# Turning V by 32x32 block transposes and a trip through DRAM instead of by TensorE transposes

## The chip, the cores and the metric

The kernel runs on one core of a Trainium2 chip. A core has a matrix engine (TensorE, called PE in the profile, with its weight loads as PEld), a vector engine (VectorE, DVE), a scalar engine (ScalarE, ACT), GpSimd (POOL) and SyncE (SP), which here only issues DMA transfers. Each engine works through its own instructions in their order and waits for others by semaphores. Work is in SBUF (128 partitions), matmul results land in PSUM banks, weights and inputs lie in DRAM. The metric is the time of one execution on the device, in microseconds (us); lower is better.

## The reference

Four layers in a row, A, B, A, B, each as x + layer(layernorm(x)), on x of 2048 tokens by 640.

Layer A is an attention with a recurrent memory. The tokens are cut into 64 segments of 32. For each segment the 8 memory rows and the 32 tokens make a sequence of 40:

```python
for s in range(n_seg):
    h = concatenate([mem, x[segment s]])            # 40 x 640
    q, k, v = h @ Wq, h @ Wk, h @ Wv                # 32 heads of 192
    p = softmax(mask(q @ k.T / sqrt(192)))
    o = (p @ v) @ Wo                                # 40 x 640
    mem = o[:8]; out[segment s] = o[8:]
```

The memory of a segment is the output of the segment before, so the 64 segments of one A layer follow each other. Layer B is a dilated sliding-window attention (window 8, dilation 2, 32 heads of 20). Weights and activations are bf16.

## The kernel before, in words

The two A layers use the same weights, and the two passes through A and B run side by side, two segments apart (LAG = 2): a step t handles segment t of the first A layer in lane 0 and segment t - 2 of the second in lane 1, 40 columns each, so NT = 80 columns. There are 64 segments and so 66 steps, and one more for the end of layer B. In steps 2 to 63, 62 in all, both lanes are at work; steps 0, 1, 64 and 65 have one lane.

A step goes through the 32 heads in 8 quads of 4 heads (768 columns of each of Wq, Wk, Wv). For quad i, `step` emits: K (`a_k`: `proj`, 30 matmuls of 128x128 weights by 80 columns, L297, then ScalarE copies into KF and Kz), Q (`a_q`, VectorE copy into QT, L316), P.V of the quad before (`a_pv`), V (`a_v`: 30 matmuls, VectorE copy into vT, L342), the output projection of the quad five back (`a_o`, L415), the normalisation of the quad before (`a_norm`, VectorE, L398 to L400), the scores S (`a_s`, L363, L364, then the exponential on ScalarE, L366) and the mask (`a_mask`, VectorE, L372). Pieces of layer B for the segment before stand between them. Quad 7 has a tail of its own: the last P.V, and the output projections of quads 3 to 7, whose result gives the memory rows of the next step.

All projections leave their result transposed: head columns on partitions, tokens along the free axis. P.V needs V with tokens on partitions. `a_vt` turns it: six PE transposes of 128 columns (L351) into one PSUM bank and one VectorE copy to Vt (L353), emitted after K of the next quad, for each of the 8 quads of a two-lane step. In one-lane steps most quads compute V with tokens on partitions at once (`a_v_rows`, L331).

P.V (L384) takes Vt as weights, with columns of ones for the sums of the softmax. ScalarE forms logarithm and exponential of these sums (R, L388, L390) and VectorE multiplies (`a_norm`).

The order on every engine, SP included, is the order of emission (a manual schedule). An instruction waits for all that it needs, and those behind it on its engine wait too.

The weights of layer A are 64 halves of 128x1920 (two for each quad and each of K, Q, V, O). 41 of them stay in SBUF; `resident_halves` picks the other 23, evenly over the step by PE work, and these are loaded again in every step into a ring of 4 buffers. `used` frees a buffer when its half has been used last, and `prefetch` then emits the next load on SP, in two pieces of 240 KB (L249), each of which waits for PE to be done with the buffer. The DMAs of SP take eight completion semaphores in turn. The loads of x (L652) and the stores of the result (L655) go through the ACT queue.

Of the kernel before, what the change touches and what calls it, by code (L numbers as in the profile page):

```python
# [28 lines left out]
LAG = 2  # L29
OLAG = 5  # L30
EPS = 1e-5

# [10 lines left out]
N_HALVES = 64  # L43
N_RES = 41
RING = 4
# [3 lines left out]

def half_order():  # L50

    quad = 15 * (NT + MM)
    other = [2 * NX * NC, 2 * NC * NC * NX, NC * NC * NX + 18 * NX, NC * P + 18 * NX, 8 * NX, 8 * NX,
             3 * P + NC * NC * NX, 2 * NX * NC]
    order = []
    for i in range(NQUAD):
        for kind in "kqv":
            order += [((kind, i, h), quad) for h in range(2)]
        last = order.pop()
        order.append((last[0], last[1] + 16 * (NT + MM) + 6 * (P + MM) + other[i]))  # L60
        for j in ([i - OLAG] if i < NQUAD - 1 else range(i - OLAG, NQUAD)):
            if j >= 0:
                order += [(("o", j, h), quad) for h in range(2)]
    return order
# [14 lines left out]
class Kernel:  # L79
    def __init__(self, ctx, tc, A_x, A_mem0, A_Wq, A_Wk, A_Wv, A_Wo, B_wqkv, B_wo, out):  # L80
        self.tc = tc
        self.nc = tc.nc
        self.x = A_x
        self.mem0 = A_mem0
        self.out = out
        self.n_seg = A_x.shape[0]
        self.wsrc = {"k": A_Wk, "q": A_Wq, "v": A_Wv, "o": A_Wo}
        pool = lambda name, bufs, **kw: ctx.enter_context(tc.tile_pool(name=name, bufs=bufs, **kw))
        self.cp = pool("consts", 1)
        self.wres = pool("wres", 1)  # L90
        self.wring = pool("wring", RING)
        self.ap1 = pool("act1", 1)
        self.ap2 = pool("act2", 2)
        self.bp = pool("bact", 1)
        self.ebp = pool("ebp", 4)
        self.otp = pool("otp", OLAG)
        self.xp = pool("xio", 1)
        self.ps_big = pool("ps_big", 1, space=PSUM)
        self.ps_one = pool("ps_one", 1, space=PSUM)
        self.ps_two = pool("ps_two", 1, space=PSUM)  # L100
        self.units = {}
        order = half_order()
        self.resident = resident_halves(order)
        streamed = [u for u, _ in order if u not in self.resident]
        self.kept = streamed[:4]
        self.kept_uses = {u: 0 for u in self.kept}
        second = streamed[4:7] + [("b", part, 0) for part in range(3)] + streamed[7:8] + [("b", 3, 0)] + streamed[8:]
        self.loads = [u for u, _ in order] + second + streamed * (self.n_seg + LAG - 2)
        self.ring_free = RING
        self.n_loaded = 0  # L110
        self.B_wqkv, self.B_wo = B_wqkv, B_wo
        self.build_consts()

    def build_consts(self):
# [23 lines left out]

        self.hT = pers("hT", [P, NC * NT + 88], 1)[0]
        self.KF = pers("KF", [P, 4 * NT + 48], 1)[0]  # L140
        self.Kz = pers("Kz", [P, 4 * NT + 48], 1)[0]
        self.Vt = pers("Vt", [P, 2 * VH], 1, zero=False)[0]
        nc.vector.memset(self.Vt[:], 1.0)
        self.vT = pers("vT", [P, 6 * NT + 48], 1)[0]
        nc.vector.memset(self.xin[0][:, 1], 0.0)
        nc.vector.memset(self.xin[1][:], 0.0)
# [139 lines left out]
    def proj(self, kind, i, t):  # L286
# [4 lines left out]
        w = [self.units[kind, i, h] for h in range(2)]  # L291
        mem_last = kind == "k" and i == 0
        order = [(n, c) for c in range(NC) for n in range(6)] if mem_last else [(n, c) for n in range(6) for c in range(NC)]
# [29 lines left out]
    def a_v_rows(self, i, t):  # L323

        nc = self.nc
        w = [self.units["v", i, h] for h in range(2)]
        vt = self.Vt[0:NT, :].rearrange("p (a b c) -> p a b c", a=2, b=2)
        for h in (1, 0):
            ps = self.big("ps_vr", ((2, 3) if i == 1 else (0, 2))[1 - h])
            for c in range(NC):  # L330
                nc.tensor.matmul(ps[:, 0:2 * DH], lhsT=self.hT[:, NT * c:NT * c + P], rhs=w[h][:, c, :], start=(c == 0), stop=(c == NC - 1))  # L331
            (nc.scalar.copy if i == 0 and h else nc.vector.tensor_copy)(out=vt[:, h, :, 0:DH], in_=ps[0:NT, 0:2 * DH].rearrange("p (b c) -> p b c", b=2))
        self.used("v", i)

    def a_v(self, i, t):
# [4 lines left out]
        nc = self.nc  # L340
        ps = self.proj("v", i, t)
        nc.vector.tensor_copy(out=self.cols(self.vT[:, 0:6 * NT].rearrange("p (a n) -> p a n", a=6)), in_=self.cols(ps[:, 0:6 * NT].rearrange("p (a n) -> p a n", a=6)))  # L342

    def a_vt(self):

        if self.v_rows:
            return
        nc = self.nc
        ps = self.ps_big.tile([P, 6, P], BF16, name="ps_vt", tag="bank2")
        for n in range(6):  # L350
            nc.tensor.transpose(out=ps[:, n, :], in_=self.vT[:, NT * n:NT * n + P], identity=self.ident[:])  # L351
        vt = self.Vt
        nc.vector.tensor_copy(out=vt[0:NT, :].rearrange("p (a b c) -> p a b c", a=2, b=2)[:, :, :, 0:DH],  # L353
                              in_=ps[0:NT].rearrange("p (a b) c -> p a (b c)", a=2).rearrange("p a (b c) -> p a b c", b=2))

# [18 lines left out]

    def a_pv(self):


        nc = self.nc
        em, vt = self.em, self.Vt
        ops = self.ps_two.tile([P, 2, 512], F32, name="ps_o", tag="o")  # L380
# [441 lines left out]
    def step(self, t):  # L822
# [4 lines left out]
        if t == T:  # L827
            return self.b_alone(b)
        for i in range(NQUAD - 1):
            self.a_k(i, t)  # L830
            if b is not None and i == 6:
                self.b_norm(1)
            if i >= 1:
                self.a_vt()
            if b is not None and i == 1:
# [6 lines left out]
            if b is not None:  # L842
                self.b_first(b, i)
            if i >= 1:
                self.a_pv()
            if b is not None and i == 6 and self.one_lane():
                self.b_ot()
            self.a_v(i, t)
            if b is not None:
                self.b_second(b, i)  # L850
            if i >= OLAG:
                self.a_o(i - OLAG)
# [5 lines left out]
            if b is not None and i == 0:  # L858
                self.b_ln(b)
            self.a_mask()  # L860
            if b is not None and i == 0:
                self.b_ln_rstd()
# [10 lines left out]
        self.a_k(7, t)  # L873
        self.a_vt()
        self.a_q(7, t)
        if nt < T:
            self.ln1_sums(nt)
        self.a_pv()
        self.a_v(7, t)
        self.a_o(7 - OLAG)  # L880
        self.a_norm(6)
        self.a_s()
        self.a_vt()
        self.a_mask()
        self.a_o(8 - OLAG)
        self.a_o(9 - OLAG, slice(0, NC), False)
        if nt < T:
            self.ln1(nt)
        self.a_pv()
        if nt < T:  # L890
# [53 lines left out]
def _lay_out(name, a):  # L944
# [3 lines left out]
    if name == "A_mem0":  # L948
        return a.reshape(NM, NC, P).transpose(2, 1, 0)
    if name in ("A_Wq", "A_Wk", "A_Wv"):  # L950
        return a.reshape(NC, P, NQUAD, 2, QE // 2).transpose(2, 1, 3, 0, 4).reshape(NQUAD, P, 2 * HALF)
# [37 lines left out]
```

## Time and profile before

| | |
|---|---|
| median of the runs (3) | 3126.81 us, 3123.92 to 3128.7 |
| profiled execution: span | 3128.7 us; no other time of it is listed |
| PE busy, PEld busy | 98%, 97% |
| DVE, ACT, POOL busy | 76%, 59%, 18% |
| mean share of the 16 DMA engines between 1000 and 2000 us | 0.76 to 0.78 |
| PE transposes of V (ps_vt, L351) | 5% of the chain, 504 groups of six |
| VectorE copies vT (L342), Vt (L353) | 653 ns and 554 ns, 504 times each |
| weight pieces on SP (240 KB) | 3.7 to 4.0 us to landing, median by tensor |
| granted clock | 0.993 |

The times of the runs are device times. The profile is one execution; its span is from its first to its last instruction. "Busy" is the time in which an engine has an instruction at work. In lines of groups and of the timeline, a name such as `vT<-ps_v` is the tile written and the tile read, an L number is the line of the kernel, and "x6" merges six instructions; the start of the next line on an engine, not the end of one, tells its rate, since instructions overlap. A name such as w_ring<-in_A_Wv_dram is a DMA. The chain is followed back from the last instruction to what each one waited for.

### The profile page before, as it was taken

How to read it: one execution, taken by the hardware profiler on the slowest of the kernel's cores; microseconds unless marked ns; L12 is line 12 of the kernel's file. 1: busy time of each engine (PE TensorE's matmuls, PEld its weight loads, DVE VectorE, ACT ScalarE, POOL GpSimd, SP SyncE). 2: the span in 40 equal slices, each digit the busy share in tenths (PEclk: the TensorE clock that was granted, in tenths of full speed). 3: DMA queues.
4: the chain of work that ended last, by engine and by line, in shares of the span. 5: the costliest groups of instructions: out<-in, count | busy, mean ns of one | idle time of the engine just before them, and what ended most of it. 6: DMA issues, size and time to landing. Idle time of an engine off the chain costs nothing.

```text
span 3128.7 us, 187179 instructions
## 1 busy us (share of the span) xinstructions
PE 3079.1 (98%) x83454; PEld 3030.8 (97%) x83454; DVE 2369.5 (76%) x6009; ACT 1845.1 (59%) x5612; POOL 553.2 (18%) x1028
## 2 busy tenths in 40 slices
PE   6999999999999999999999999999999999999998
PEld 4899999999999999999999999999999999999997
DVE  3677777777777777777777777777777777877776
ACT  2556656656656656656656656656656656655654
POOL 2111111111111111111111111111111111111121
PEclk7999999999999999999999999999999999999999
DMA  9877777777777777777777777777777777777776
GB/s 392 287 246 248 246 246 239 250 243 246 249 244 249 246 246 250 247 247 247 247 246 248 248 245 249 250 246 245 250 246 248 249 244 249 250 243 250 248 251 219
DMA packets 452970, 785.02 MB, mean 251 GB/s; under 512 B 58560, under 2 KB 444352, under 8 KB 452160
## 3 DMA queue, kind: packets, MB, share of 16 engines
q1 hardware_dynamic: 438480, 767.84, 76.4%
q8 instruction: 652, 10.68, 1.4%
q10 hardware_dynamic: 13680, 5.21, 0.7%
q14 instruction: 158, 1.29, 0.1%
HBM read 770.22 MB, written 2.62 MB: 247 GB/s over the span
## 4 chain that ended last, share of the span: by engine, by line
PE 96%; DMA 3%; issue 1%; ACT 0%; DVE 0%; SPq 0%; ACTq 0%
PE ps_k L297 18%; PE ps_acc L415 18%; PE ps_q L297 17%; PE ps_v L297 17%; PE ps_vt L351 5%; PE ps_o L384 5%; PE ps_s L363 2%; PE ps_s L364 2%; PE ps_bs L581 2%; PE ps_bk L529 2%; PE ps_by L640 2%; PE ps_bq L529 1%; PE ps_bv L529 1%; PE ps_vr L331 1%; PE ps_bo L607 1%
## 5 line engine op out<-in xcount | busy, mean ns | idle before, releaser
L388 ACT ACTIVATE R<-ps_o 64x160 f32<-64x160 f32 (+1 forms) x2112 | 620.1, 294 | 338.4 <-PE ps_o L384 122.8
L297 PEld LDWEIGHTS <-w_ring 128*128 128x128 bf16 x16470 | 676.6, 100 | 18.7 <-issue 5.3
L297 PE MATMUL ps_q<-hT,w_q 128*128 128x80 bf16 (+1 forms) x12870 | 541.1, 201 | 4.8 <-DMA w_q<-in_A_Wq_dram 4.2
L566 POOL TENSOR_TENSOR QX<-QB,hmask 128x448 bf16<-128x448 bf16 (+2 forms) x325 | 304.5, 945 | 1338.2 <-ACT QB L544 1025.1
L297 PEld LDWEIGHTS <-w_q 128*128 128x128 bf16 x12870 | 493.8, 100 | 6.0 <-DMA w_q<-in_A_Wq_dram 5.3
L309 ACT CAST KF<-ps_k 128x320 bf16<-128x320 f32 (+1 forms) x528 | 218.5, 414 | 414.7 <-PE ps_k L297 399.1
L415 PE MATMUL ps_acc<-OT,w_o 128*128 128x80 bf16 (+1 forms) x9900 | 458.9, 201 | 3.7 <-DMA w_o<-in_A_Wo_dram 2.3
L342 DVE CAST vT<-ps_v 128x480 bf16<-128x480 f32 (+1 forms) x504 | 329.3, 653 | 166.2 <-PE ps_v L297 148.1
L316 DVE CAST QT<-ps_q 128x480 bf16<-128x480 f32 (+1 forms) x528 | 337.5, 639 | 119.7 <-PE ps_q L297 116.5
L297 PE MATMUL ps_v<-hT,w_v 128*128 128x80 bf16 (+1 forms) x9480 | 423.7, 201 | 4.1 <-issue 2.4
L415 PEld LDWEIGHTS <-w_o 128*128 128x128 bf16 x9900 | 393.2, 100 | 5.4 <-DMA w_o<-in_A_Wo_dram 2.9
L297 PE MATMUL ps_k<-hT,w_k 128*128 128x80 bf16 (+1 forms) x7920 | 373.5, 201 | 2.9 <-DMA w_k<-in_A_Wk_dram 2.7
L297 PEld LDWEIGHTS <-w_v 128*128 128x128 bf16 x9480 | 371.6, 100 | 4.9 <-issue 2.9
L297 PE MATMUL ps_k<-hT,w_ring 128*128 128x80 bf16 (+1 forms) x7860 | 370.5, 201 | 5.4 <-issue 3.4
L366 ACT ACTIVATE E<-ps_s 80x320 bf16<-80x320 f32 (+1 forms) x528 | 220.7, 418 | 241.4 <-PE ps_s L364 240.1
L398 DVE TENSOR_TENSOR OT<-ps_o,R 128x320 bf16<-128x320 f32 (+1 forms) x528 | 254.1, 481 | 135.4 <-ACT R L390 115.7
L297 PEld LDWEIGHTS <-w_k 128*128 128x128 bf16 x7920 | 321.5, 100 | 3.7 <-DMA w_k<-in_A_Wk_dram 3.1
L353 DVE COPY Vt<-ps_vt 80x768 bf16<-80x768 bf16 x504 | 279.0, 554 | 56.4 <-PE ps_vt L351 44.5
L415 PE MATMUL ps_acc<-OT,w_ring 128*128 128x80 bf16 (+1 forms) x5940 | 307.9, 201 | 1.5 <-issue 1.1
L297 PE MATMUL ps_v<-hT,w_ring 128*128 128x80 bf16 (+1 forms) x5640 | 264.8, 202 | 0.8 <-DMA w_ring<-in_A_Wv_dram 0.7
L372 DVE TENSOR_TENSOR E<-E,maskA 80x320 bf16<-80x320 bf16 (+1 forms) x528 | 207.0, 392 | 64.7 <-ACT E L366 54.0
L390 ACT ACTIVATE R<-R 128x320 f32<-128x320 f32 (+1 forms) x528 | 244.1, 462 | 16.7
(159 smaller groups left out, 4932.2 us busy)
## 6 DMA issues: line engine op xcount, KB each, us to landing
w_ring<-in_A_Wk_dram SPq DMA_DIRECT2D x1036, 240.0 KB, 3.7
w_ring<-in_A_Wo_dram SPq DMA_DIRECT2D x780, 240.0 KB, 3.8
w_ring<-in_A_Wv_dram SPq DMA_DIRECT2D x776, 240.0 KB, 4.0
w_ring<-in_A_Wq_dram SPq DMA_DIRECT2D x390, 240.0 KB, 4.0
w_q<-in_A_Wq_dram SPq DMA_DIRECT2D x5, 960.0 KB, 11.0
w_v<-in_A_Wv_dram SPq DMA_DIRECT2D x6, 480.0 KB, 11.3
w_ring<-in_A_Wk_dram SPq DMA_DIRECT2D x6, 480.0 KB, 10.2
w_ring<-in_A_Wo_dram SPq DMA_DIRECT2D x6, 480.0 KB, 11.3
```

Of the source, the lines that this page charges most:

```text
L297: nc.tensor.matmul(ps[:, NT * n + self.c0:NT * n + self.c1], lhsT=w[n // 3][:, c, P * (n % 3):P * (n % 3 + 1)], rhs=hT[:, NT * c + self.c0 ...
L309: nc.scalar.copy(out=kf, in_=pv[:, :, 0:3:2, :])
L316: self.nc.vector.tensor_copy(out=self.cols(qt[:]), in_=self.cols(ps[:, 0:6 * NT].rearrange("p (a n) -> p a n", a=6)))
L342: nc.vector.tensor_copy(out=self.cols(self.vT[:, 0:6 * NT].rearrange("p (a n) -> p a n", a=6)), in_=self.cols(ps[:, 0:6 * NT].rearrange("p ...
L353: nc.vector.tensor_copy(out=vt[0:NT, :].rearrange("p (a b c) -> p a b c", a=2, b=2)[:, :, :, 0:DH], in_=ps[0:NT].rearrange("p (a b) c -> p ...
L366: nc.scalar.activation(out=self.cols(e[0:NT]), in_=self.cols(sv[0:NT]), func=ACT.Exp, scale=float(DH) ** -0.5)
L372: nc.vector.tensor_tensor(out=self.cols(e[0:NT]), in0=self.cols(e[0:NT]), in1=self.cols(self.maskA[0:NT, :]).unsqueeze(1).to_broadcast([NT ...
L388: nc.scalar.activation(out=self.cols(r[r0:r0 + 64, :, j]), in_=self.cols(src), func=ACT.Ln)
L390: nc.scalar.activation(out=rf, in_=rf, func=ACT.Exp, scale=-1.0)
L398: nc.vector.tensor_tensor(out=oc[:, :, 0:3:2], in0=ov[:, :, 0:4:3], in1=r, op=ALU.mult)
L415: nc.tensor.matmul(self.cols(acc[:, k]), lhsT=w[m // 3][:, m % 3, P * c:P * (c + 1)], rhs=self.cols(ot[:, m]), start=(i == 0 and m == 0 an ...
L566: self.nc.gpsimd.tensor_tensor(out=qx[:, 0:nh, self.on], in0=self.qb[:, c, self.on].unsqueeze(1).to_broadcast([P, nh, n]), in1=self.hmask[ ...
```

## The change

In two-lane steps, V of quads 2 to 7 is turned in another way. The V projection runs two quads ahead: V of quad 2 at the start of the step, V of quad i + 2 in quad i. Its PSUM result is copied to vS (one buffer). `v_blocks` turns 32x32 blocks on VectorE, 128 partitions by 576 elements, from vS into vB (one buffer). `v_send` stores vB to a DRAM buffer (two buffers), and `v_fetch` brings it back in three loads, of token rows 0 to 31, 32 to 63 and 64 to 79, in runs of 192 elements, straight into Vt, of which there are now two buffers. The store and the three loads are issued on SP. Quads 0 and 1 keep the PE transposes. So that the loads have long runs, the columns of Wv of quads 2 to 7 are reordered on the host, and one-lane steps write their V in the same order.

One resident half less fits, 40 instead of 41, so that 24 halves are streamed per step; two-lane steps stream them in the order of the new use.

```diff
-N_RES = 41
+N_RES = 40
...
+        if two_lanes:
+            units = [("v", VLAG)] * (i == 0) + [("k", i), ("q", i)]
+            units += [("v", VLAG + i)] * (1 <= i < NQUAD - VLAG) + [("v", i)] * (i < VLAG)
...
+        self.v_by_dma = not self.one_lane() and i >= VLAG
+        if self.v_by_dma:
+            nc.vector.tensor_copy(out=self.vS[:, 0:6 * NT], in_=ps[:, 0:6 * NT])
+            return
...
+    def v_blocks(self, i):
+        src = self.vS[:]
+        src = bass.AP(src.tensor, src.offset, [list(src.ap[0]), [VB, 3], [NT, 6], [1, VB]])
+        self.nc.vector.transpose(out=self.vB[:].rearrange("p (b n c) -> p b n c", b=3, n=6), in_=src)
+
+    def v_send(self, i):
+        self.v_sent[i] = self.vdp.tile([P, 3 * DH], BF16, name="v_rows")
+        self.nc.sync.dma_start(out=self.v_sent[i][:], in_=self.vB[:])
+
+    def v_fetch(self, i):
+        rows = self.v_sent.pop(i)[:].rearrange("(h i) c -> i h c", h=4)
+        for b in range(3):
+            n = min(VB, NT - VB * b)
+            vt = self.Vts[i % 2][VB * b:VB * b + n, :].rearrange("p (h c) -> p h c", h=4)
+            self.nc.sync.dma_start(out=vt[:, :, 0:DH], in_=rows[0:n, :, DH * b:DH * (b + 1)])
...
+        ahead = not self.one_lane()
+        if ahead:
+            self.a_v(VLAG, t)
         for i in range(NQUAD - 1):
             self.a_k(i, t)
+            if ahead and i == 0:
+                self.v_blocks(VLAG)
...
             self.a_q(i, t)
...
+            if ahead and i >= 1:
+                self.v_send(i + 1)
             if i >= 1:
-                self.a_pv()
+                self.a_pv(i - 1)
...
-            self.a_v(i, t)
+            if not ahead or i == 0:
+                self.a_v(i, t)
+            elif i < NQUAD - VLAG:
+                self.a_v(i + VLAG, t)
             if b is not None:
                 self.b_second(b, i)
+            if ahead and i == 1:
+                self.a_v(i, t)
...
             self.a_mask()
+            if ahead and 1 <= i < NQUAD - VLAG:
+                self.v_blocks(i + VLAG)
+            if ahead and i >= 1:
+                self.v_fetch(i + 1)
...
-        self.a_v(7, t)
+        if not ahead:
+            self.a_v(7, t)
```

## The prediction

> **What bounds the kernel now.** I read the page's busy shares first, then the chain, then single steps of the loop in the timeline, then the DMA landings. In the page, TensorE (PE) is busy for 98% of the span and is 96% of the chain that ended last; VectorE (DVE) follows at 76%.
>
> ```profile
> PE 3079.1 (98%) x83454; PEld 3030.8 (97%) x83454; DVE 2369.5 (76%) x6009; ACT 1845.1 (59%) x5612; POOL 553.2 (18%) x1028
> PE 96%; DMA 3%; issue 1%; ACT 0%; DVE 0%; SPq 0%; ACTq 0%
> ```
>
> A two-lane step (there are 62, t = 2 to 63) takes 47.4 us. The table of stretches, cut at the first K matmul of quads 3, 4, 5 of one step (columns: length, then busy PE, PEld, DVE, ACT, POOL, granted clock, DMA share, GB/s), shows no PE slack and a VectorE almost as full:
>
> ```profile
> 1503.07:1507.98 4.91, 4.91 (x124) 4.77 (x121) 4.27 (x12) 4.18 (x13) 1.91 (x2) 1.00 0.76 240
> 1507.98:1512.11 4.13, 4.13 (x113) 4.13 (x112) 3.31 (x9) 3.14 (x10) 0.00 (x0) 1.00 0.81 250
> 1512.11:1517.75 5.64, 5.64 (x164) 5.64 (x161) 5.20 (x13) 3.46 (x11) 0.00 (x0) 1.00 0.79 263
> ```
>
> In the timeline, the six transposes of V of one quad and what follows them on PE; then, from SyncE's queue (SP), the issue of one streamed half (two pieces) each:
>
> ```profile
> 1504.11 0.36 PEld L351 LDWEIGHTS <-vT 128*128 128x128 bf16 x6
> 1504.43 0.62 PEld L297 LDWEIGHTS <-w_q 128*128 128x128 bf16 x15
> ...
> 1508.71 0.81 SPq L249 DMA_DIRECT2D w_ring<-in_A_Wv_dram  x2
> 1509.63 0.84 SPq L249 DMA_DIRECT2D w_ring<-in_A_Wo_dram  x2
> ```
>
> Last, the time from issue to landing, for the 80 KB stores of the output (ACT queue), for the 40 KB loads of x (ACT queue), and for the 240 KB weight pieces (SP queue), in this order:
>
> ```profile
> DMA to landing us min/median/max: 1.6/3.5/4.7
> ```
> ```profile
> DMA to landing us min/median/max: 1.9/2.9/4.3
> ```
> ```profile
> DMA to landing us min/median/max: 2.5/3.8/6.4
> ```
>
> The reader is to see that a transfer costs about 3 us of latency however small it is, and that a quad lasts only 4 to 5.6 us.
>
> **Part 1, the transposes leave PE.** 1504.43 - 1504.11 = 0.32 us per quad, six quads: -1.92 us per step, all on the path. Were nothing else to move, 62 x 1.92 = 119 us would go.
>
> **Part 2, the PE order.** V of quad i+2 is projected in quad i; the same 30 matmuls stand elsewhere. With 0.32 us taken out of the starts of the trace and the V projections moved, a step that begins with V of quad 2 at 0 has: end of Q of quad 2 at 13.9, K of quad 3 at 16.7, of 4 at 21.3, of 5 at 25.1, of 6 at 30.4, of 7 at 35.6, and P.V of quad 7 at 40.8. Two dependences lose cover:
> - Head. VectorE still works at the two sums of ln_s when the step starts (until 2.5 us after it) and then has the copy of V (L342's row: 0.56 from one start to the next) and the block transpose ahead of QT of quad 0. QT and ln_h come some 1.3 us later than now (1490.90 to 1492.0 in the trace), PE only 1.08 later: +0.2 us per step, bounds 0 and 0.8.
> - Tail. V of quad 7 (1.08) and its transposes (0.32) no longer stand between P.V of quad 6 and P.V of quad 7. The mask of quad 7 waits for the normalisation of quad 6 (done at 1530.2), ends 0.35 later, at 1530.55; P.V would be wanted at 1529.85 (1527.12, plus O of quad 2 with 1.08, S 0.28, O of quad 3 with 1.08, the first O matmuls of quad 4 and the statistics, 0.29). +0.8 us with the semaphore, if nothing later holds it.
>
> **Part 3, VectorE.** Six PSUM copies of 554 ns go, six block transposes of 128x576 come. The trace has none. Low 0.46 us (row of the 128x512 bf16 mask: 459 ns), high 1.26 (rate of the reduction: 700 ns for 320); I take 0.70, near the 128x480 casts (654 ns). Quads 3 to 5 then hold 12.8 - 3 x 0.55 + 3 x 0.70 = 13.2 us of VectorE in 13.7 us: just hidden. The VectorE page of the Trainium skill (VectorE: DVE Perf Modes, The three transpose paths) has 311 ns for a 128x128 transpose; scaled by columns that is an estimate of 1.4 us, by which these quads would be VectorE's by 1.6 us; no run here shows the instruction.
>
> **Part 4, DMA bytes.** 24 halves are streamed instead of 23, and 768 packets of 1152 bytes and 1920 of 384 bytes come per step. By the page's queues a packet of 1751 bytes takes 87 ns (76.4% of 16 x 3128.7 us over 438480) and one of 381 bytes 26 ns; 1152 bytes interpolate to 60. (256 x 87 + 768 x 60 + 1920 x 26) / 16 = 7.4 us of 47: the DMA share goes from 0.77 to about 0.93. Not over the limit, so I charge nothing; if it queues, landings lengthen, which part 5 prices.
>
> **Part 5, SP's queue, which decides.** SP issues in order. Of each quad it now issues a store and three loads, and the first load waits until the store has landed; the halves behind it wait with it. The block transpose of the next quad waits for the same landing (vB is one buffer), and VectorE's next QT copy stands behind that. From the store for quad 3, which SP reaches when the half released by Q of quad 2 is issued (13.9 + 0.8 = 14.7), the order is:
> - store 3, loads 3, two halves; store 4, a half (during the wait), loads 4, two halves; store 5, loads 5, two halves: three rounds of L + 3 x 0.41 + 2 x 0.82 = L + 2.87 each, with L the store's landing from its issue;
> - store 6, two halves (during the wait), loads 6, one half: L + 2.05;
> - store 7, loads 7, landed: L + 1.23 + 2.5 = L + 3.7 (load landing 2.9 from the x row, its issue 0.4 counted already).
>
> Sum 5L + 14.4 us, in which PE gets from 14.7 to 40.8, that is 26.1. PE stalls by 5L - 11.7 per step, at P.V of quad 7 at the latest, mostly before (Q of quad 6 on its half, S of quad 5 on QT). Bounds of L: 1.6 (the quickest store) and 3.8 (median weight piece; the store rides behind such pieces). I take 3.2, between the two ACT rows, 2.9 and 3.5: stall 4.3 us. It contains the tail's 0.8.
>
> **Sum.** -1.92 + 0.2 + 4.3 = +2.6 us per step, x 62 = +160 us. The traced execution's own time is not listed apart from its span, 3128.7; the median of the runs is 1.9 less. 3128.7 + 160 - 1.9 = 3287 us. The four one-lane steps, start and end stay: the same 64 halves are loaded first.
>
> **The rivals.**
> - Faster: the store lands fast. Below L = 2.3 the rounds fit, and only head and tail remain: -1.92 + 0.2 + 0.8 = -0.92 x 62 = -57: 3070 us. The whole change breaks even at 5L - 11.7 + 0.2 = 1.92, L = 2.68. For it: the quickest store took 1.6. Against: the weight pieces in the very same queue never took less than 2.5. The DMA page of the Trainium skill (DMA: Bandwidth & Descriptors, Anatomy of one DMA) gives 2.0 us plus bytes over 436 GB/s for one transfer (fitted on transfers that GpSimd issues), an estimate of 2.3 us for the store's 147 KB; by that rule this rival is the outcome, about 3070 us; the rows above show more on loaded queues. Chance 0.18.
> - No change to measure (within 0.2%, 6 us, about what three runs that spread over 4.8 us can tell): L between 2.66 and 2.70, or head and tail worse: 0.04.
> - Slower than forecast: the share of 0.93 queues, and the store takes what a weight piece takes, 3.8. 5 x 3.8 - 11.7 = 7.3; (7.3 + 0.2 - 1.92) x 62 = +346: 3473 us. For it: two halves are always issued just ahead of stores 4, 5, 6. Against: a stalled PE releases halves later, which empties the queue. 0.24.
> - VectorE becomes the bound, SP does not: a transpose of 1.26 us. Quads 3 to 5 exceed PE by 1.2; with head 0.8 and tail 0.8: +0.9 x 62 = +55: 3182 us. Against: the mask rows at 0.8 ns per element. 0.04.
> - The forecast, L from 2.7 to 3.5 (3128 to 3380 us): 0.50.
> - That the transposes stay is excluded: the changed program has 62 x 6 x 6 = 2232 fewer PE matmuls.
>
> **How the numbers follow.** Faster 0.18; same 0.04; slower 0.50 + 0.24 + 0.04 = 0.78. The range, 3066 to 3475, reaches from the faster rival (with half of its cases below) to the slowest one; about 0.1 lies outside at each end. The forecast's own range is 3128 to 3380.
>
> **What will show it.** Right: the transposes of PE at 132 groups instead of 504; in SP's own waits, the loads of V waiting for the landing of v_rows, about 2.8 us each and 372 times; PE waits for w_ring in Q of quads 4 and 6 and for QT; VectorE's block transpose waiting for the store; DMA share about 0.9; steps of 50 us. Wrong: if v_rows lands within 2.3 us, or if SP's waits for it end before PE frees the next half, no stall follows and steps take 46.5 us. If the transposes take over 1 us, part 3 was wrong. If the stalls stand at the head or the tail alone, part 2 decides.

## The result, and the profile after

| | before | after |
|---|---|---|
| median of the runs | 3125.51 us (4 runs, 3123.92 to 3128.7) | 4130.5 us (4 runs, 4117.21 to 4140.47) |
| ratio, 95% interval | | 1.3213, 1.3186 to 1.3241 |
| span of the profiled execution | 3128.7 us | 4125.5 us |
| one two-lane step (median of the trace, first long O group to the next) | 46.72 us | 62.46 us |
| mean granted clock | 0.993 | 0.911 |

The change costs 1005 us. The forecast was 3287 us, slower by 160; the time lies far outside the range of 3066 to 3475. The sign and the place were right, the size was not.

The page of the changed kernel, busy times and chain:

```profile
PE 3333.5 (81%) x81222; PEld 3208.3 (78%) x81222; DVE 2372.0 (57%) x6011; ACT 1865.2 (45%) x5612; POOL 550.1 (13%) x1028
...
PE 44%; DMA 30%; DVE 15%; issue 4%; ACT 3%; SPq 3%; DVEq 0%; POOL 0%; ACTq 0%; POOLq 0%
```

PE fell from 96% of the chain to 44%; DMA rose from 3% to 30%. PE has 2232 matmuls fewer and is still busy for 254 us more: it runs slower (below). The table of stretches of one step, cut at the first K matmul of quads 3, 4, 5, 6 and 7 (length, busy PE, PEld, DVE, ACT, POOL, granted clock, DMA share, GB/s):

```profile
2028.33:2035.58 7.25, 5.09 (x117) 4.62 (x115) 4.21 (x12) 4.79 (x14) 1.86 (x2) 1.00 0.53 161
2035.58:2042.61 7.03, 4.13 (x107) 3.89 (x106) 3.62 (x10) 3.33 (x10) 0.00 (x0) 1.00 0.71 237
2042.61:2052.28 9.67, 6.24 (x157) 5.75 (x154) 4.83 (x13) 2.99 (x9) 0.00 (x0) 0.95 0.54 156
2052.28:2062.40 10.12, 7.30 (x138) 7.20 (x136) 4.33 (x12) 4.10 (x12) 0.00 (x0) 0.72 0.85 272
```

The quads that took 4.91, 4.13 and 5.64 us take 7.25, 7.03 and 9.67. No resource is full in the first three: PE, VectorE and DMA all have slack, as when everything stands in a line behind one latency. The waits of the changed kernel name it, first those of SP, then those of the engines (total us, times, longest us):

```profile
SPq L400 <- DMA v_rows<-vB: 950.9, 340, 6.7
```
```profile
DVE vB L387 <- DMA v_rows<-vB: 902.8, 248, 5.8
...
PE ps_s L409 <- DVE QT L329: 258.0, 124, 4.2
...
PE ps_bt L675 <- DVE On L668: 205.3, 54, 5.9
...
PE ps_bo L653 <- DVE On L668: 122.3, 62, 3.4
```

Both SP (its first load of V) and VectorE (its next block transpose) wait for the landing of the store, some 900 us each, and PE waits for the VectorE results queued behind. The store's landing, and the block transpose:

```profile
v_rows<-vB SPq DMA_DIRECT2D x372, 144.0 KB, 4.5
```
```profile
L387 DVE STREAM_TRANSPOSE vB<-vS 128x576 bf16<-128x576 bf16 x372 | 288.8, 776 | 904.9 <-DMA v_rows<-vB 902.8
```

L, the store's time from issue to landing, is 4.5 us in the median; the prediction took 3.2 and had 3.8 as its upper bound. The chain through quads 3 to 6 of one step, followed back from the end, has the store in every round. Between a landing and the next store it names VectorE (vB, then QT or On), PE, and the issue of weights on SP:

```profile
2027.89 5.04 DMA v_rows<-vB
2033.02 0.78 DVE vB L387
...
2036.28 4.44 DMA v_rows<-vB
2040.81 0.78 DVE vB L387
...
2044.71 4.35 DMA v_rows<-vB
...
2052.32 4.33 DMA v_rows<-vB
```

In SP's own timeline of one such round, the queue is seen to stand still and then to issue back to back:

```profile
2036.28 0.43 SPq L392 DMA_DIRECT2D v_rows<-vB  x1
2036.80 0.91 SPq L262 DMA_DIRECT2D w_ring<-in_A_Wq_dram  x2
2040.73 1.99 SPq L400 DMA_DIRECT2D Vt<-v_rows  x3
2042.82 0.85 SPq L262 DMA_DIRECT2D w_ring<-in_A_Wv_dram  x2
2043.71 0.90 SPq L262 DMA_DIRECT2D w_ring<-in_A_Wo_dram  x2
2044.71 0.38 SPq L392 DMA_DIRECT2D v_rows<-vB  x1
```

The store lands at 2040.72 (2036.28 + 4.44); the first load starts 0.01 us later; from there to the next store no pause is longer than 0.1 us. So on SP this round is landing plus issues, as the prediction wrote it. The chain goes through VectorE in the same time; which of the two sets the pace is for the experiments.

### The profile page after: what moved, and what is told of

It reads as the page before. It is cut to its first block, busy times and chain, and to the rows that moved or that the text cites. A ratio compares the mean times of both kernels' runs of the same rounds, so it can differ in the third digit from the quotient of the medians.

```text
span 4125.5 us, 185373 instructions
## 1 busy us (share of the span) xinstructions
PE 3333.5 (81%) x81222; PEld 3208.3 (78%) x81222; DVE 2372.0 (57%) x6011; ACT 1865.2 (45%) x5612; POOL 550.1 (13%) x1028
## 4 chain that ended last, share of the span: by engine, by line
PE 44%; DMA 30%; DVE 15%; issue 4%; ACT 3%; SPq 3%; DVEq 0%; POOL 0%; ACTq 0%; POOLq 0%
DMA v_rows<-vB 27%; PE ps_acc L461 10%; PE ps_k L310 8%; PE ps_v L310 7%; PE ps_q L310 6%; DVE vB L387 4%; SPq L262 2%; DVE QT L329 2%; PE ps_o L430 2%; ACT R L434 2%; DVE On L668 2%; PE ps_s L409 2%; PE ps_by L686 2%; DVE OT L444 1%; PE ps_s L410 1%
## 5 line engine op out<-in xcount | busy, mean ns | idle before, releaser
L310 PEld LDWEIGHTS <-w_ring 128*128 128x128 bf16 x17550 | 768.0, 104 | 93.5 <-DMA w_ring<-in_A_Wq_dram 30.7
L387 DVE STREAM_TRANSPOSE vB<-vS 128x576 bf16<-128x576 bf16 x372 | 288.8, 776 | 904.9 <-DMA v_rows<-vB 902.8
L461 PE MATMUL ps_acc<-OT,w_o 128*128 128x80 bf16 (+1 forms) x9900 | 523.2, 207 | 2.5 <-DMA w_o<-in_A_Wo_dram 1.9
L310 PE MATMUL ps_v<-hT,w_v 128*128 128x80 bf16 (+1 forms) x10350 | 482.4, 202 | 4.1 <-issue 3.5
L409 PE MATMUL ps_s<-QT,KF 128*128 128x80 bf16 (+1 forms) x2112 | 242.5, 213 | 258.0 <-DVE QT L329 258.0
L310 PEld LDWEIGHTS <-w_v 128*128 128x128 bf16 x10350 | 419.6, 100 | 4.7 <-issue 3.9
L461 PE MATMUL ps_acc<-OT,w_ring 128*128 128x80 bf16 (+1 forms) x5940 | 379.2, 210 | 33.2 <-DMA w_ring<-in_A_Wo_dram 31.9
L410 PEld LDWEIGHTS <-Kz 128*128 128x128 bf16 x2112 | 186.9, 107 | 277.0 <-issue 248.1
L310 PEld LDWEIGHTS <-w_k 128*128 128x128 bf16 x7920 | 366.8, 111 | 9.6 <-issue 2.9
L461 PEld LDWEIGHTS <-w_ring 128*128 128x128 bf16 x5940 | 291.1, 106 | 43.1 <-DMA w_ring<-in_A_Wo_dram 41.7
L484 POOL TENSOR_TENSOR sq<-xin 128x320 bf16<-128x320 bf16 x65 | 46.7, 719 | 2027.9 <-PE ps_by L686 1864.7
```

Of the source, the lines that this page charges most:

```text
L310: nc.tensor.matmul(ps[:, NT * n + self.c0:NT * n + self.c1], lhsT=w[n // 3][:, c, P * (n % 3):P * (n % 3 + 1)], rhs=hT[:, NT * c + self.c0 ...
L387: self.nc.vector.transpose(out=self.vB[:].rearrange("p (b n c) -> p b n c", b=3, n=6), in_=src)
L409: nc.tensor.matmul(self.cols(sv[:, h]), lhsT=kf[:, NT * h:NT * h + P], rhs=self.cols(qt[:, 3 * pr + 2 * j]), start=True, stop=False)
L410: nc.tensor.matmul(self.cols(sv[:, h]), lhsT=kz[:, NT * h:NT * h + P], rhs=self.cols(qt[:, 3 * pr + 1]), start=False, stop=True)
L461: nc.tensor.matmul(self.cols(acc[:, k]), lhsT=w[m // 3][:, m % 3, P * c:P * (c + 1)], rhs=self.cols(ot[:, m]), start=(i == 0 and m == 0 an ...
```

## The experiments

Theory 1: SP's in-order queue, held by the first load until the store has landed, sets the rounds. Theory 2: VectorE is held by the same landing, because vB is one buffer, and PE waits behind VectorE (that is what the waits of PE name). A third candidate: the bytes and issues of the trip, whatever waits for it.

**Second block buffer** (quads 4 and 6 use vT, free by then): VectorE no longer waits.

```diff
+    def vb_of(self, i):
+
+        return self.vT if i in (4, 6) else self.vB
...
-        self.nc.sync.dma_start(out=self.v_sent[i][:], in_=self.vB[:])
+        self.nc.sync.dma_start(out=self.v_sent[i][:], in_=self.vb_of(i)[:])
```

> Two buffers for the transposed blocks (quads 4 and 6 use the buffer of vT, free by then), so that VectorE's block transpose no longer waits for the landing of the store just issued; SyncE's order is as in the changed kernel. If VectorE's wait is what costs (902.8 us of it in the changed kernel, with the copy of QT and the normalisation of layer B behind it), most of the 1005 us goes: below 3450 us. If SyncE's queue is what costs, as the prediction had it, its rounds stay: with a landing of 4.5 us, 5 x 4.5 - 11.7 = 10.8 us of stall per step and about 3690 us or more.

Measured: 4048.98 us (4041.71 to 4056.26), ratio 1.295 (1.2894 to 1.3006), 82 us less than after. VectorE's wait for v_rows is gone, SP's is not (717.3 + 278.8 us), and PE now waits for weights instead:

```profile
SPq L404 <- DMA v_rows<-vB: 717.3, 248, 5.6
...
SPq L404 <- DMA v_rows<-vT: 278.8, 124, 3.5
```
```profile
PE ps_q L310 <- DMA w_ring<-in_A_Wq_dram: 327.5, 258, 4.2
```

So what ended last in PE's waits (QT, On) did not set the pace alone: take it away, and the weights are nearly as late.

**Loads later** (each quad's loads emitted one quad later, just ahead of the next store; vB one buffer): by then the store has landed.

```diff
+            if ahead and i >= 2:
+                self.v_fetch(i)
             if ahead and i >= 1:
                 self.v_send(i + 1)
...
-            if ahead and i >= 1:
-                self.v_fetch(i + 1)
```

> One buffer for the blocks, but the three loads of a quad's V are issued one quad later, just ahead of the next store, when their store has landed, so that SyncE does not wait with weights behind it. If SyncE's queue costs, this is near 3100 us. If VectorE's wait for the one buffer costs, the stores leave earlier than in the changed kernel but VectorE still waits some 2 us in four or five quads: 3400 to 3800 us.

Measured: 3649.38 us (3643.66 to 3655.1), ratio 1.1672 (1.1627 to 1.1716), 481 us less than after. SP's waits for v_rows fall from 951 to 70 us. But the loads now land too late for P.V (`PE ps_o L430 <- DMA Vt<-v_rows: 271.6` us in the waits), and VectorE still waits 365 us for vB.

**Both edits.**

> Both edits together: two block buffers, loads one quad later. If these two waits are all that the change loses, only its gain (1.92 us per step) and the head and tail (0.2 and 0.8 us) remain: about 3070 us, faster than before. If DMA load (one more half, small packets) or late V costs too, it is above 3126 us.

Measured: 3689.82 us (3689.3 to 3690.35), ratio 1.1801 (1.1767 to 1.1835). VectorE's wait for the store is gone and SP's is 77 us, and it is not faster than the later loads alone: P.V waits for Vt, which is loaded one quad ahead of its use with a landing of 4.0 us:

```profile
PE ps_o L434 <- DMA Vt<-v_rows: 335.6, 196, 4.4
```

So here moving the wait along the queue trades late weights for late V. To price the parts, the next kernels take them away one at a time.

**No trip**: no store, no loads; the projections two quads ahead, the copies, the block transposes and the 24th streamed half stay.

```diff
-            if ahead and i >= 1:
-                self.v_send(i + 1)
...
-            if ahead and i >= 1:
-                self.v_fetch(i + 1)
```

> The store to DRAM and the three loads are left out, so P.V of quads 2 to 7 in two-lane steps multiplies with an old Vt; everything else of the change stays (order of V, block transposes, 24 streamed halves). It prices parts 1 to 3 of the prediction alone: -1.92 + 0.2 + 0.8 us per step, 3070 us. If the block transposes (778 ns measured) or the missing cover in the tail cost more, it is above that; above 3126 us the change loses even without its trip.

Measured: 3146.21 us (3142.76 to 3147.26), ratio 1.0059 (1.0036 to 1.0082). Without the DMAs of its trip the change loses 19 us, where parts 1 to 3 of the prediction have it win 57. In the waits of PE, with few waits for a DMA, two new ones stand:

```profile
PE ps_st L513 <- POOL ln_h L494: 29.9, 60, 0.6
PE ps_bt L675 <- DVE On L668: 22.2, 54, 0.7
PE ps_st L513 <- POOL ln_h L495: 18.1, 62, 0.4
```

**Ceiling**: the kernel before without the six transposes and their copies, nothing else changed.

```diff
+        if not self.one_lane() and self.vt_n % 8 >= 2:
+            self.vt_n += 1
+            return
+        self.vt_n += not self.one_lane()
         nc = self.nc
         ps = self.ps_big.tile([P, 6, P], BF16, name="ps_vt", tag="bank2")
```

> The kernel before, with the six PE transposes of V of quads 2 to 7 and the PSUM copies that follow them left out in the two-lane steps (V of those quads is stale); nothing moved, nothing added. It is the ceiling of what the change can win. If the 0.32 us of each quad was on the path with nothing behind it: 62 x 1.92 = 119 us less, about 3008 us. Rival: the waits that the run without the trip showed (the statistics of the next layer-norm on GpSimd, the transposes of layer B on On) come from the shorter PE stream itself and eat most of it: 3070 to 3127 us.

Measured: 3033.7 us (3024.09 to 3037.89), ratio 0.9681 (0.9657 to 0.9705). The transposes of PE, with their copies, are worth 93 to 96 us by the medians (92 to 107 by the interval of the ratio), not 119; the median step falls by 1.49 us, not 1.92. Where the other 0.43 us stay was not traced to one place. Everything else in the change has to cost less than this, or it loses.

**Loads that don't depend on the store**: the loads read a DRAM tile written once; stores, bytes, issues and their order stay.

```diff
-        rows = self.v_sent.pop(i)[:].rearrange("(h i) c -> i h c", h=4)
+        self.v_sent.pop(i)
+        rows = self.v_old[:].rearrange("(h i) c -> i h c", h=4)
```

> The changed kernel, but the loads of V read a tile of DRAM that was written once at the start (V of quads 2 to 7 is that constant), while the store goes on as before to its own tile: the same bytes, the same issues in the same order, and the block transpose still waits for the store's landing (one vB), but no load waits for a store, so SP's queue is held by nothing. If SP's hold is the main cost, what is left is the loop landing 4.4 + transpose 0.8 + issue 0.4 = 5.6 us against quads of 4.1 to 5.6 us: some 2 to 3 us a step over the 3146 us without the trip, 3270 to 3330 us. If the queue's issues and bytes by themselves are the cost: above 3500 us.

Measured: 3515.8 us (3514.56 to 3517.05), ratio 1.123 (1.1208 to 1.1253): 615 us less than after. SP's hold at the landing is the largest single part, but the expected 3270 to 3330 was missed.

**The same with the second block buffer**: next to nothing waits for a landing of the store any more (SP 9 us in all).

> As the run before, with a second block buffer for quads 4 and 6: now nothing waits for a landing, but every store, load and byte is still there, from the same queue. If the trip's price is only its waits: 3146 us (the run without the trip) plus at most 1 us a step, 3146 to 3210 us. If the DMA share of about 0.93 or SP's 24 more issues per step delay the weights: 3300 us or more, with PE waits for w_ring.

Measured: 3410.96 us (3406.7 to 3415.22), ratio 1.0895 (1.087 to 1.092). Another 105 us go with VectorE's wait. It is still 265 us above the kernel without the trip, with a store that is hardly waited for: the third candidate is real as well. PE's waits show weights, and Vt at P.V, mostly of quads 6 and 7, where the loads are issued behind halves of the weights:

```profile
PE ps_acc L470 <- DMA w_ring<-in_A_Wo_dram: 65.6, 110, 2.3
...
PE ps_q L314 <- DMA w_ring<-in_A_Wq_dram: 49.0, 100, 2.1
...
PE ps_o L439 <- DMA Vt<-v_old: 41.9, 42, 3.0
```

**The same, with the DMAs cut to a corner** (16 rows per store, 4 per load): the issues stay, of the trip's bytes 86% go (100.8 MB more than without the trip become 13.9) and of its packets 82%.

```diff
-        self.nc.sync.dma_start(out=self.v_sent[i][:], in_=self.vb_of(i)[:])
+        self.nc.sync.dma_start(out=self.v_sent[i][0:16], in_=self.vb_of(i)[0:16])
...
-            n = min(VB, NT - VB * b)
+            n = 4
```

> The run in which nothing waits for a landing (3411 us), with the same stores and loads issued at the same places, but each moves a corner only: 16 of the store's 128 rows, 4 of the rows of each load (V of quads 2 to 7 is that constant corner). Issues stay, nine tenths of V's bytes go. If SP's time at 24 more issues a step is what costs the 265 us over the run without the trip: about 3380 to 3410 us. If it is the bytes on the DMA engines (share about 0.93, weights landing later): 3150 to 3200 us.

Measured: 3205.46 us (3203.19 to 3207.72), ratio 1.0247 (1.0226 to 1.0267). So 206 of the 265 us go with the bytes and packets, which were not told apart, and 59 with the issues and what is left of the bytes. Between 1000 and 2000 us the DMA share is 0.81 in the run without the trip, 0.81 with the corner and 0.86 with all the bytes. It doesn't reach 1.00, but PE's first two waits for w_ring in the last fence are three and six times those with the corner (21.4 and 7.6 us in the same two rows).

**Store sent early** (two block buffers, each store right behind its block transpose): a kernel that computes V, with a whole quad for the landing.

```diff
-            if ahead and i >= 1:
-                self.v_send(i + 1)
...
                 self.v_fetch(i + 1)
+            if ahead and 1 <= i < NQUAD - VLAG:
+                self.v_send(i + VLAG)
```

> The changed kernel with two block buffers and the store sent half a quad earlier, right behind its block transposes, the loads where they are: the store has a whole quad (4.1 to 5.6 us) to land before SP reaches the load, instead of half of one, and the loads keep a quad and a half. If the head-of-line wait at a landing of 4.4 us is what costs: SP's waits for v_rows fall from 340 of 6.7 us at most to about 1 us each, and the time to 3150 to 3300 us. Rival: SP now waits for VectorE's transposes instead, and the weights behind it are as late: 3500 us or more.

Measured: 3504.62 us (3496.75 to 3512.5), ratio 1.1195 (1.1159 to 1.123). It is the best of the kernels that do all of the change's work, 626 us better than it. The wait for the landing is nearly gone, but the expected 3150 to 3300 was missed. The rival that was named has its share, since SP now waits for VectorE's block transposes; that its 3500 came out is partly luck, for the bytes and issues, 265 us in the run above, were in neither price:

```profile
SPq L396 <- DVE vB L391: 226.2, 127, 3.5
...
SPq L404 <- DMA v_rows<-vB: 60.5, 98, 2.2
```

Its stores land in 3.3 us, against 4.5 in the changed kernel.

**The same, with the loads issued by GpSimd.**

```diff
-            self.nc.sync.dma_start(out=vt[:, :, 0:DH], in_=rows[0:n, :, DH * b:DH * (b + 1)])
+            self.nc.gpsimd.dma_start(out=vt[:, :, 0:DH], in_=rows[0:n, :, DH * b:DH * (b + 1)])
```

> The kernel with two block buffers and the early store (3505 us), its loads of V issued from GpSimd's queue in place of SP's. SP then has 6 more issues a step in place of 24, and waits for no landing. If SP's queue is the scarce thing: 3250 to 3350 us, no waits of SP for v_rows, weights on time. If the bytes are: 3450 us or more. Rival: GpSimd now stands in order before the landing, and the layer norm's sums behind it come late: PE waits for ps_st, 3550 us.

Measured: 4296.09 us (4291.46 to 4300.72), ratio 1.3733 (1.3706 to 1.3761), slower than the change itself. The rival that was named is in PE's waits (GpSimd stands before the landing, and its own work behind it is late), but its price, 3550 us, was far too low:

```profile
PE ps_o L434 <- DMA Vt<-v_rows: 352.4, 156, 5.9
PE ps_st L517 <- POOL ln_h L498: 243.7, 62, 6.2
PE ps_bs L631 <- POOL QX L616: 156.1, 85, 4.3
```

So late weights are traded for late V (Vt) and for late work of GpSimd, the layer norm (ln_h) and layer B's masked Q (QX). Two more things changed with it and were not told apart: the 1116 loads take GpSimd 0.55 us each to issue, and SP's waits for the block transposes grew to 499.1 (vB) and 214.9 us (vT). Loads from the ACT queue were not tried.

**No trip, and no block transposes.**

```diff
-            if ahead and 1 <= i < NQUAD - VLAG:
-                self.v_blocks(i + VLAG)
```

> The run without the trip (3146 us), its six block transposes per step left out as well (V of quads 2 to 7 is stale): what is left is the order of PE, the 24th streamed half and the six copies of V. If VectorE's 0.77 us per block is what made layer B's transposes wait for On (0.62 us in the step looked at): 62 x 0.6 = 38 us less, about 3108 us. If the time lies in the order (the statistics waiting for GpSimd at the tail, 1.1 us a step, and the head's 0.4): 3135 to 3146 us.

Measured: 3103.39 us (3101.42 to 3105.76), ratio 0.992 (0.9903 to 0.9936). The wait of ps_bt for On, 22.2 us, is gone; the block transposes cost 43 us in all. What is left over the ceiling, 70 us, is the order and the 24th half, neither of which was tried alone; the waits of ps_st are still there, 24.1 and 17.8 us.

**No trip, GpSimd's sums emitted ahead of K of quad 7.**

```diff
+        if nt < T:
+            self.ln1_sums(nt)
         self.a_k(7, t)
         self.a_vt(6)
         self.a_q(7, t)
-        if nt < T:
-            self.ln1_sums(nt)
```

> The run without the trip (3146 us; V of quads 2 to 7 is stale), with GpSimd's sums for the next step's layer norm put ahead of K of quad 7 instead of behind Q of quad 7. If what the shorter tail waits for is the statistics (gaps of 0.69 and 0.44 us ahead of and between the two ps_st matmuls in the step looked at), 62 x 1.13 = 70 us go: about 3076 us. If the mask of quad 7 is late next, as the prediction had it (P.V of quad 7, 0.8 us): 3100 to 3125 us. If GpSimd can't start earlier since it waits for a buffer of layer B: no change.

Measured: 3148.41 us (3144.79 to 3151.41), ratio 1.0078 (1.0061 to 1.0095): nothing moved, and the waits of ps_st stay (31.4 and 18.1 us). The expected 3076 was wrong. No change had been named too, but for another reason, a wait of GpSimd for a buffer of layer B. The emission is not what starts GpSimd. In the timeline of the run without the trip, then of before, the sums start as soon as VectorE has written layer B's output into xin:

```profile
1527.71 0.89 PE L686 MATMUL ps_by<-OTB,wb_sb 128*128 128x64 bf16 x25
1530.27 0.33 DVE L692 TENSOR_TENSOR xin<-ps_by,x 128x160 bf16<-128x160 f32 x1
...
1530.72 0.72 POOL L484 TENSOR_TENSOR sq<-xin 128x320 bf16<-128x320 bf16 x1 [17.50 <-ACT Kz L324]
...
1534.18 0.22 PE L513 MATMUL ps_st<-ln_h,ones 128*128 128x128 bf16 x1 [0.52 <-POOL ln_h L494]
```
```profile
1523.55 0.90 PE L640 MATMUL ps_by<-OTB,wb_sb 128*128 128x64 bf16 x25
1525.02 0.33 DVE L646 TENSOR_TENSOR xin<-ps_by,x 128x160 bf16<-128x160 f32 x1
...
1525.48 0.72 POOL L438 TENSOR_TENSOR sq<-xin 128x320 bf16<-128x320 bf16 x1 [18.52 <-issue]
...
1528.96 0.43 POOL L449 TENSOR_TENSOR ln_h<-ln_s,ln_h 128x128 bf16<-128x128 f32 x1
...
1531.59 0.28 PE L467 MATMUL ps_st<-ln_h,ones 128*128 128x128 bf16 x2
```

In both, sq starts 0.13 us after xin is written (1530.27 + 0.33, 1525.02 + 0.33); the releaser printed beside it (Kz, issue) is another in each. Before, the sums are done 2.2 us ahead of ps_st. After the change V of quad 7 and two groups of transposes no longer stand between ps_by and ps_st, and VectorE writes xin 1.67 us after ps_by is done, not 0.57. Counted from start to start and less the usual spacing of the matmuls, the statistics are then late by 0.69 us, and by 0.44 between the two ps_st. These 1.13 us x 62 would be the 70 us that the kernel without block transposes has over the ceiling, but no run took them away.

**The ladder.** Each rung takes one thing away from the rung above (the kernel before, beside them on four chip sessions, was at 3125.5 to 3130 us):

| kernel | us | what the step down is worth |
|---|---|---|
| after | 4130.5 | |
| loads don't wait for the store | 3515.8 | SP's hold at the landing: 615 |
| and a second block buffer | 3411.0 | VectorE's wait on vB: 105 |
| and a corner of the bytes | 3205.5 | most bytes and packets of the trip: 206 |
| and no trip | 3146.2 | 24 more issues a step, the corner's bytes: 59 |
| and no block transposes | 3103.4 | VectorE's 0.77 us each: 43 |
| before, without transposes | 3033.7 | order of PE, 24th half: 70 |
| before | 3127 | PE transposes and their copies: -93 |

A price holds for its place on the ladder: VectorE's wait was worth 82 us with SP's hold in place and 105 without it. The rows come from four sessions, so each carries some 5 us.

## Why the prediction was right or wrong

**Part 5 was right in its mechanism and wrong in its sizes; these make the error.** The step that failed is the term L, the store's landing: 3.2 us was taken, with 3.8 as the upper bound, and 4.5 came. SP's waits for v_rows were forecast as 2.8 us each, 372 times, and are 950.9 us over 340, 2.8 us each. Of the step in the chain above (V of quad 2 at 2011.34 to the next at 2072.84, 61.5 us), each term of the sum can be set beside its measurement (predicted P.V of quad 7 to the end: the median step 46.72 - 1.92 + 0.2 - 40.8; the 47.4 us of the prediction was one step, longer than the median):

| term | predicted | measured |
|---|---|---|
| step start to store 3 | 14.7 | 16.55 (2027.89) |
| five landings, 5L | 5 x 3.2 = 16.0 | 5.04 + 4.44 + 4.35 + 4.33 + 4.40 = 22.56 |
| the rest of the five rounds | 3 x 2.87 + 2.05 + 3.7 = 14.4 | 3.35 + 3.99 + 3.26 + 2.38 + 4.98 = 17.96 |
| P.V of quad 7 to the end | 4.2 | 4.43 |
| sum | 49.3 | 61.5 |

- L is the main term, +6.6 of the +12.2 us. The reason given for 3.2 ("between the two ACT rows") took rows of a queue where at most one other transfer was in flight at the issue, with 2 weight pieces on SP's queue (medians of before); the store of the changed kernel goes out behind 4. It goes out right behind two weight halves and lands with them: the last piece ahead of it at 2035.80 takes 4.47 us, the store behind it 4.44. What it takes goes with the weight pieces still in flight when it is issued (last section); the row to take was the weight piece, in the same queue, and even its median was too little. The Trainium skill (DMA: Bandwidth & Descriptors, Anatomy of one DMA), with 2.0 us plus bytes over 436 GB/s for a transfer that GpSimd issues, gives an estimate of 2.3. That is nearer to a store with nothing ahead of it, 1.8 us in the median of 39 early ones; the changed kernel has none such.
- The issues are +2.3, in the first four rounds: seven DMAs of a round were charged at 0.41 us; they start 0.47 us apart, and single ones take over 1 us (the second of the three loads that take 1.99 us in the timeline: 1.14).
- The last round is +1.3, and not by issues: its third load takes 3.4 us to land where 2.9 was taken, and P.V starts 0.7 us after that landing, since the mask of quad 7 is late (part 2).
- Step start to store 3 is +1.9: store 2 has a round of its own, which the sum left out. SP issues without a pause from its landing at 2022.43 to store 3.

The table is SP's account, and up to store 6 the chain runs through its landings. The fifth landing did not set the end of this step: the loads of quad 7 have landed at 2067.69, when PE is just ready for their P.V. Four landings are +5.4 of the +6.6.

With L = 4.5 alone the prediction's own formula gives 5 x 4.5 - 11.7 = 10.8, (10.8 + 0.2 - 1.92) x 62 = 563 us more than before, of 1005; the smaller terms are the rest of this step, and steps differ. Of the signs, the waits of PE for QT came (258.0 us), those for weights in Q hardly (22.7 us, until VectorE no longer waited: 327.5).

**That block transposes wait for the same landing** was said, but not priced. It is worth 82 us while SP is held and 105 when it is not; its 902.8 us of waiting cost so much less because SP waits for the same landing.

**Part 1**: 93 us instead of 119. The transposes did leave: 792 matmuls ps_vt in place of 3024.

**Part 2, head and tail.** The tail was right for the changed kernel: P.V of quad 7 waits for its mask (the E of L418) in 61 of the 62 steps, 0.7 us each, against 0.8 forecast.

```profile
PE ps_o L430 <- DVE E L418: 40.8, 61, 0.7
```

Without the trip, when PE comes sooner, this wait is absent and the statistics behind layer B's output are late instead (0.69 and 0.44 us). There the order and the 24th half cost 70 us of the ladder, against (0.2 + 0.8) x 62 = 62 forecast for the order; that the two are near is partly luck, as another wait makes up the tail. The head's 0.2 was not looked at alone.

**Part 3.** One block transpose takes 776 ns; 0.70 was taken. The estimate of 1.4 us scaled from the Trainium skill (VectorE: DVE Perf Modes, The three transpose paths) is far off: 576 columns cost 2.5 times its 311 ns for 128. "Just hidden" was wrong: the six cost 43 us without the trip, 22 of which stand in the wait of layer B's ps_bt for On.

**Part 4 charged nothing for the bytes, and they cost 206 us** with their packets, once the waits for the store are gone, though the share between 1000 and 2000 us only goes from 0.81 to 0.86. The proviso that queueing would show in part 5 did not cover this: here the store's landing is hardly waited for. In the changed kernel itself the share is 0.70 over the same stretch, not the 0.9 that was to show: the stalls stretch the step.

**The rivals.** The faster one needed L under 2.3 and fell with L. The rival "slower than forecast" named the right reason, two halves ahead of the store, and was bounded at 3.8. That bound is what made the range too narrow: a median of a row of before, where the share is 0.77, was taken as an upper end for a transfer that stands behind more pieces in its queue. The same row's longest was 6.4.

None of the versions run here comes near before: the bytes, issues, block transposes and order add up to 206 + 59 + 43 + 70 = 378 us with hardly a wait for a store, against 93 that PE gains. A trip for fewer quads, or through another queue than SP's and GpSimd's, was not tried.

## What to carry to other kernels

Work that is moved from the bounding engine to a DMA round trip must be priced with the landing of a transfer that stands behind its neighbours in the same queue, taken from the upper half of that queue's landings, and once for each in-order queue that waits for it. Before such a change, run the kernel with the work left out: here the ceiling was 3%, and the bytes and packets of the trip alone cost more than twice that. A wait that ends last on the busiest engine need not set the pace; give it a buffer, and see whether another late thing stands behind it.

## What the runs showed of the hardware

**A stall of PE over about 2 us can cost half as much again.** In the table of stretches for the changed kernel, a stall and what follows it (granted clock is the number ahead of the last two):

```profile
2055.70:2058.51 2.81, 0.00 (x1) 0.00 (x0) 1.66 (x5) 0.00 (x0) 0.00 (x0) 0.92 1.01 368
2058.51:2061.32 2.81, 2.81 (x41) 2.81 (x41) 0.63 (x1) 2.12 (x7) 0.00 (x0) 0.50 0.83 253
2061.32:2067.46 6.14, 6.14 (x179) 6.14 (x176) 3.18 (x9) 3.53 (x11) 3.44 (x9) 0.99 0.53 150
```

After 2.8 us without a matmul PE runs at half its clock for 2.8 us, which do the work of 1.4, then at full. Not every such stall does this. Earlier in the same step PE is idle for 2.7 us ahead of 2042.33 and goes on at full clock:

```profile
2038.38:2042.33 3.95, 1.24 (x35) 1.14 (x32) 1.49 (x3) 1.66 (x5) 0.00 (x0) 1.00 0.65 232
2042.33:2046.46 4.13, 4.13 (x114) 4.04 (x114) 2.12 (x6) 2.25 (x8) 0.00 (x0) 1.00 0.67 188
```

From the starts of the matmuls between 300 and 2900 us (mean spacing of the first, second and third 30 behind a gap, median over the gaps; gaps with another of over 0.8 us in those 90 are left out; "at half clock" where the median spacing of the first 30 is over 50 ns):

| gap before (start to start) | times | at half clock | first 30 | next 30 | next 30 |
|---|---|---|---|---|---|
| 0.8 to 1.0 us | 43 | 0 | 35.7 ns | 35.8 | 35.8 |
| 1.5 to 2.0 us | 17 | 2 | 36.1 | 39.8 | 34.8 |
| 2.0 to 2.5 us | 19 | 10 | 64.9 | 48.8 | 36.0 |
| 2.5 to 3.0 us | 22 | 18 | 65.2 | 52.7 | 33.2 |
| 3.0 to 3.5 us | 19 | 13 | 65.2 | 54.7 | 33.1 |
| over 3.5 us | 30 | 29 | 69.2 | 62.2 | 38.5 |

The Trainium skill (TensorE: Matmul & The Clock Gate, Part 1: The HAM clock gate) has the two speeds and the return after sustained work, and puts the fall behind an idle window of about 3.4 us. The trace agrees on the two speeds; here half of the gaps of 2.0 to 2.5 us were already enough, and nearly all of those over 3.5 us. With the same 81222 matmuls PE is busy for 3333.5 us in the changed kernel (clock 0.911) and for 3128.4 us in the one whose loads don't wait for the store (clock 0.969), 205 us less. How much of that is on the path was not tried.

**The same 144 KB store takes 1.8 to 4.8 us in the median, and longer the more is in flight ahead of it.** From the traces, from 300 us on, the median from issue to landing by the number of weight pieces (240 KB, same queue) that had been issued and had not landed when the store was issued (times in brackets; 1 piece and more than 5 are left out):

| kernel | 0 | 2 | 3 | 4 | 5 |
|---|---|---|---|---|---|
| after | - | 2.92 (4) | 3.03 (50) | 4.47 (203) | 4.80 (82) |
| store sent early | 1.80 (39) | 3.06 (72) | 3.06 (93) | 3.92 (129) | - |
| loads by GpSimd | 1.91 (78) | 2.65 (84) | 3.07 (62) | 3.29 (69) | 3.94 (21) |

So L is no constant of the transfer: it goes with what stands ahead of it in the queue. Single stores scatter (2.8 to 6.4 us behind 4 pieces in the changed kernel), and no run changed this alone, so that it is the cause is not shown. The L under 2.3 of the faster rival is there, in a queue that the stores of this change never find: their quickest took 2.7 us.
